# The keys' projections of a fused attention and mixture-of-experts kernel: three float32r products of split operands in place of one float32 product

## Chip, cores and metric

The kernel runs on one core of one Trainium2 chip. The metric is the device time of that core in microseconds (us), as the median of several executions. Shares of a difference are given against the 980.4 us of the kernel before.

## The reference

The reference is a chain of three parts: a linear attention with random features, a dense feed-forward layer, and a layer of eight experts with a capacity. Only the first part is touched. Cut to what matters:

```python
batch, n_heads, seq, head_dim, n_features = 4, 8, 576, 64, 128
scale = 1.0 / np.sqrt(np.sqrt(D))
def phi(x):                                       # x: q * scale or k * scale
    proj = np.einsum('bhsd,md->bhsm', x, omega)   # the projection
    sq = np.sum(x * x, axis=-1, keepdims=True) / 2.0
    h = proj - sq
    h = h - np.max(h, axis=-1, keepdims=True)
    return np.exp(h) / np.sqrt(m)
q_p, k_p = phi(q * scale), phi(k * scale)
kv = np.einsum('bhsm,bhsd->bhmd', k_p, v)
z = np.sum(k_p, axis=2)
num = np.einsum('bhsm,bhmd->bhsd', q_p, kv)
den = np.einsum('bhsm,bhm->bhs', q_p, z)[..., None] + 1e-06
attn = num / den
x = dense_layer(attn)                             # w_in, w_out: float64, 512 x 2048
return experts(x)                                 # 8 experts, 288 tokens each
```

## The kernel before

**The stages of the span.** The attention takes about the first 200 us, the dense layer runs to about 630 us, and the routing and the experts fill the rest. The work of the attention is cut into 36 units of 1024 rows (eight blocks of 128 rows of a head): 18 units of keys first, then 18 units of queries. The list `seq` (line 340) holds them in this order. So the attention has a **key stretch** and a **query stretch**.

**One unit.** `st_T` (line 208) transposes the unit's rows on TensorE (four transposes, line 212) into one bank of PSUM, the tile `tp`, and ScalarE copies it to `tH` in SBUF (line 215). GpSimd squares the rows and adds the two halves of each row's squares (lines 218 and 220). `st_TL` (line 225) has VectorE sum the squares (line 233); for a unit that is split it also forms the low part `tL` = `tp` minus `tH` on VectorE (line 230). `st_proj` (line 236) then multiplies four blocks of the transposed rows with the 128 x 256 matrix of features. If the unit has no `tL`, each block is one float32 matmul against `bdfl` (line 247). If it has one, each block is three float32r matmuls, high by high, high by low, low by high, in the helper `mm3` (lines 204 to 206) against `bdH` and `bdL`. VectorE takes the row maxima (lines 253 and 255) and forms the bias of the exponential (lines 260 and 261). ScalarE computes the exponential in eight instructions (`st_exp`, line 269). A unit of keys ends with the products of `kp` and the values into `kv` (line 279), which VectorE copies out once for every half batch (line 293). A unit of queries ends with transposes (line 301), the products with `kv` (lines 314 and 319), the division on VectorE (lines 322 to 324) and transposes back (line 333).

**What sets the order.** The loop at line 386 traces step i with the stages in the order of `ORDER` (line 30): loads, a weight conversion, the transposes of unit i + 2, the projection and the exponential of unit i, then the low part and the sum of squares of unit i + 2, then the products with the values of unit i - 1. The compiler's list scheduler turns this into one fixed order of instructions for each engine, and each engine works through its own list in order. The tile `tp` has one buffer (`PA`, line 55): the transposes of the next unit wait until every reader of the last ones is done. The transposes of the queries' results use the same bank. `tH` and `tL` have three buffers each (`TH`, line 28), the projections four banks.

**The conversions beside it.** The float64 weights of the dense layer are converted to float32 on the chip, 512 columns at a time (`conv`, line 159): one load on the queue of SP, two instructions of ScalarE (lines 172 and 173), four of VectorE (lines 174 to 177) and two of GpSimd (lines 178 and 179). Twenty-two conversions are spread over the 36 steps of the attention, about two in each three steps from step 2 on (line 363).

The lines that choose the form of the projection:

```python
tH = ap.tile([P, 512], F32 if nat else F32R, tag="tH", name="tH", bufs=TH)      # 214
if not nat:                                                                     # 228
    tL = ap.tile([P, 512], F32R, tag="tL", name="tL", bufs=TH)
    nc.vector.tensor_tensor(tL, pt, tH.bitcast(F32), ALU.subtract)
if tL is None:                                                                  # 246
    nc.tensor.matmul(o, tH[:, c], bdfl, start=True, stop=True, skip_group_check=True)
else:
    mm3(o, tH[:, c], tL[:, c], bdH, bdL)
```

Of the kernel before, what the change touches and what calls it, by code (L numbers as in the profile page):

```python
# [20 lines left out]
def fused(tc, q, k, v, omega, w_in, w_out, w_gate, w1, w2, out):  # L21
# [7 lines left out]
    L1, L2, L3, LK, TA, TB, NA = 2, 3, 4, 1, 2, 2, 4  # L29
# [20 lines left out]
    with ctx:  # L50
# [9 lines left out]
        def ps(tag):  # L60
            if tag == "big":
                turn[0] += 1
                tag = ("s8", "kv", "kv")[turn[0] % 3]
            tag = TG.get(tag, tag)
            return pp.tile([P, 512], F32, tag=tag, name=tag, bufs=PA[tag])
# [56 lines left out]
        def ensure(kind, u):  # L122
            if kind == "v":
                key = (kind, u)
                if key not in held:
                    held[key] = load_v(u)
                return held[key]
            key = (kind, u[0], u[1], u[-1])
            if key not in held:
                src = {"k": k, "q": q}[kind]  # L130
                held[key] = load_mixed(src, u[1]) if u[0] == "m" else load_full(src, u[1], u[3])
            r = held[key]
            return r if u[0] == "m" else r[:, :, 2 * u[2] * D:(2 * u[2] + 2) * D]

        def quads(u, a):

            return a.rearrange("p (a j) d -> p a j d", a=2) if u[0] == "m" else a.rearrange("p j (a d) -> p a j d", a=2)
# [43 lines left out]
        def conv_in(f, pool, pool2):  # L181
            dst = wbig[f // 8].rearrange("p (c n) -> p c n", c=4)[:, :, (f % 8) * P:(f % 8 + 1) * P]
            m = 2 if wide else 1
            conv(pool, wi_src[:, :, f * P * m:(f + 1) * P * m], dst, (4, P), pool2)

        def conv_out(f, pool, pool2=None):
            conv(pool, wo_src[:, f], wbig[2 + f // 8][:, (f % 8) * 512:(f % 8 + 1) * 512], (512,), pool2)
# [20 lines left out]
        def st_T(kind, u, nat):  # L208
            src = ensure(kind, u)
            pt = ps("T")  # L210
            for j in range(4):
                nc.tensor.transpose(pt[:, j * P:(j + 1) * P],
                                    src[:, 2 * j:2 * j + 2].rearrange("p a d -> p (a d)") if u[0] == "m" else src[:, j], ident)
            tH = ap.tile([P, 512], F32 if nat else F32R, tag="tH", name="tH", bufs=TH)
            nc.scalar.copy(tH, pt)
            sq = ap.tile([P, 2, 4, D], F32, tag="sq", name="sq", bufs=2)
            sf = quads(u, src)
            nc.gpsimd.tensor_tensor(sq, sf, sf, ALU.mult)
            s2 = ap.tile([P, 2, 4, D // 2], F32, tag="s2", name="s2", bufs=2)
            nc.gpsimd.tensor_tensor(s2, sq[:, :, :, :D // 2], sq[:, :, :, D // 2:], ALU.add)  # L220
            return pt, tH, s2, nat
# [3 lines left out]
        def st_TL(st):  # L225
            pt, tH, sq, nat = st
            tL = None
            if not nat:
                tL = ap.tile([P, 512], F32R, tag="tL", name="tL", bufs=TH)
                nc.vector.tensor_tensor(tL, pt, tH.bitcast(F32), ALU.subtract)  # L230
            ns[0] += 1
            s8 = s8s[:, ns[0] % 8 * 8:(ns[0] % 8 + 1) * 8].rearrange("p (a j) -> p a j", a=2)
            nc.vector.tensor_reduce(s8, sq, AX.X, ALU.add)
            return tH, tL, s8

        def st_proj(u, tHL):
            tH, tL, s8 = tHL
            mx = ap.tile([P, 2, 4], F32, tag="mx", name="mx", bufs=2)
            pjs = []
            for hf in range(2):  # L240
                pj = ps("proj")
                for jj in range(2):
                    j = 2 * hf + jj
                    c = slice(j * P, (j + 1) * P)
                    o = pj[:, jj * 256:(jj + 1) * 256]
                    if tL is None:
# [3 lines that stand above are left out]
                p4 = pj.rearrange("p (h m) -> p h m", h=4)  # L250
                pjs.append(p4)
                if u[0] == "m":
                    nc.vector.tensor_reduce(mx[:, hf], p4, AX.X, ALU.max)
                else:
                    nc.vector.tensor_reduce(mx[:, :, 2 * hf:2 * hf + 2].rearrange("p a j -> p j a"),
                                            p4.rearrange("p (j a) m -> p j a m", a=2), AX.X, ALU.max)
            hm = ap.tile([P, 2, 4], F32, tag="hm", name="hm", bufs=2)
            bias = ap.tile([P, 2, 4], F32, tag="bias", name="bias", bufs=2)

            nc.vector.scalar_tensor_tensor(hm, s8, -SCALE * SCALE / 2.0, mx, ALU.mult, ALU.add)  # L260
            nc.vector.scalar_tensor_tensor(bias, s8, -SCALE * SCALE / 2.0, hm, ALU.mult, ALU.subtract)  # L261
            return pjs, bias

        def st_exp(u, pb):
            pjs, bias = pb
            kp = (ap if u[0] == "f" else at_p).tile([P, 2, 4, M], F32, tag="kp" + u[0], name="kp", bufs=KP if u[0] == "f" else 2)
            for s in range(8):
                i, j = at(u, s)
                nc.scalar.activation(kp[:, i, j], pjs[s // 4][:, s % 4], AF.Exp, bias=bias[:, i, j:j + 1])  # L269
            return kp  # L270
# [13 lines left out]
        def kv_of(u):  # L284
            if u[0] == "m":
                return
            _, b, rp, hg = u
            for r in range(2):
                kv_mm(b, hg, u, r, full, rp == 0 and r == 0, False)
            if rp == 1:  # L290
                rows = slice(64 * (b % 2), 64 * (b % 2) + 64)
                kv_mm(b, hg, ("m", b // 2), hg, rows, False, True)
                nc.vector.tensor_copy(kv[b][:, 4 * hg:4 * hg + 4].rearrange("p h d -> p (h d)"), kvacc.pop((b, hg))[:, 0:260])
# [46 lines left out]
        seq = [("k", u) for u in korder] + [("q", u) for u in qorder]  # L340
        n = len(seq)
        T, pj, ex, qT, nums = {}, {}, {}, {}, {}

        def need(i):
            if 0 <= i < n:
                ensure(*seq[i])

        def need_v(i):
            if 0 <= i < n and seq[i][0] == "k":
                ensure("v", seq[i][1])  # L350
# [10 lines left out]
        def stages(i):  # L361
            yield "load", lambda: (need(i + NA), need_v(i + VF - 2))
            z = next((z for z in range(NF + CE) if C0 + int(z * CS) == i), None)
            if z is not None:
                yield "conv", lambda: conv_in(z, ar, ap) if z < NF else conv_out(z - NF, ar, ap)
            if 0 <= i + TA < n:
                yield "T", lambda: T.__setitem__(i + TA, st_T(*seq[i + TA], seq[i + TA][0] == "k"))
            if 0 <= i < n:
                yield "proj", lambda: pj.__setitem__(i, st_proj(seq[i][1], T.pop(i)))
                yield "exp", lambda: ex.__setitem__(i, st_exp(seq[i][1], pj.pop(i)))  # L370
            if 0 <= i + TB < n:
                yield "TL", lambda: T.__setitem__(i + TB, st_TL(T[i + TB]))
            if 0 <= i - LK < n and seq[i - LK][0] == "k":
                def kv_():
                    u = seq[i - LK][1]
                    kps[u], vs[u] = ex.pop(i - LK), held["v", u]
                    kv_of(u)
                yield "kv", kv_
            if 0 <= i - L1 < n and seq[i - L1][0] == "q":
                yield "qT", lambda: qT.__setitem__(i - L1, st_qT(seq[i - L1][1], ex.pop(i - L1)))  # L380
            if 0 <= i - L2 < n and seq[i - L2][0] == "q":
                yield "num", lambda: nums.__setitem__(i - L2, st_num(seq[i - L2][1], qT.pop(i - L2)))
            if 0 <= i - L3 < n and seq[i - L3][0] == "q":
                yield "xT", lambda: st_xT(seq[i - L3][1], nums.pop(i - L3))

        for i in range(-TA, n + 6):
            st = dict(stages(i))
            for name in ORDER:
                if name in st:
                    st[name]()  # L390
            if i == GI:
                gate()
# [276 lines left out]
        i = 0  # L669
# [396 lines left out]
```

## Time and profile before

| what | value |
|---|---|
| runs | 980.35, 980.4 and 984.51 us, median 980.4 us |
| the profiled execution | 981.92 us |
| its span, first to last instruction | 980.1 us |
| busy over the span | PE 92%, PEld 80%, DVE 70%, ACT 50%, POOL 50% |
| key stretch, first to last projection | 9.31 to 85.86 us |
| query stretch, first projection to the last attention unit | 85.86 to about 195 us |

PE is TensorE's matmuls, PEld its weight loads, DVE is VectorE, ACT ScalarE, POOL GpSimd and SP the engine that issues most loads. The profiled execution's time holds 1.8 us around its span. Shares over the whole span mix stages that have different limits, so the stages have to be read one by one. A matmul's duration in the profile overlaps the next one's, so the cost of a matmul in a dense row is the distance between two starts.

### The profile page before, as it was taken

The numbers are of one execution on the slowest core, as the hardware profiler recorded it, in microseconds if no ns is written. First come the engines' busy times: TensorE is split into PE (matmuls) and PEld (weight loads), VectorE is DVE, ScalarE is ACT, GpSimd is POOL, SyncE is SP. The second block draws the span as 40 slices with busy tenths as digits, with TensorE's granted clock in tenths as the row PEclk, the third lists the DMA queues.
The fourth block names the chain that finished last, engine by engine and source line by source line (L and its number), as shares of the span: only waits on it lengthen the run. The fifth ranks groups of instructions, "written<-read, shape, count | busy, mean of one in ns | idle before, by whom it ended". The sixth has DMA issues, their size and how long they took to land. (4 is left out here: it accounts for less than half of the span.)

```text
span 980.1 us, 16364 instructions
## 1 busy us (share of the span) xinstructions
PE 901.3 (92%) x5753; PEld 783.2 (80%) x5753; DVE 685.0 (70%) x1789; ACT 491.2 (50%) x1082; POOL 485.6 (50%) x447
## 2 busy tenths in 40 slices
PE   7999899999899999999999997886999899898996
PEld 6998788877678888878878886655888888787996
DVE  4779888778875662694369239967888887976442
ACT  5767788865454544534543455322344343342552
POOL 6669765346653533545444556352433533525442
PEclk9999899999999999999999999996999999998999
DMA  8855522012301000000010001014624624615500
GB/s 196 226 157 158 153 89 82 2 69 82 151 1 36 8 1 1 33 12 0 1 44 1 1 0 44 1 47 171 197 86 136 221 74 148 221 43 203 197 25 25
DMA packets 74850, 81.89 MB, mean 84 GB/s; under 512 B 27016, under 2 KB 59784, under 8 KB 74640
## 3 DMA queue, kind: packets, MB, share of 16 engines
q1 hardware_dynamic: 71696, 71.41, 22.9%
q0 software_dynamic: 3072, 9.44, 3.2%
q8 instruction: 45, 0.74, 0.3%
q14 instruction: 37, 0.30, 0.1%
HBM read 71.39 MB, written 9.45 MB: 82 GB/s over the span
## 5 line engine op out<-in xcount | busy, mean ns | idle before, releaser
L501 POOL TENSOR_TENSOR iL<-W,iH 128x512 fp32r<-128x512 f32 x80 | 114.9, 1437 | 103.7 <-ACT iH L500 88.6
L924 POOL TENSOR_TENSOR iL<-We,iH 128x512 fp32r<-128x512 f32 x63 | 84.8, 1349 | 135.2 <-ACT iH L921 127.9
L204 PE MATMUL kv<-xH,iH 128*128 128x512 f32 (+2 forms) x376 | 134.2, 357 | 5.0 <-DVE gLk L545 3.3
L206 PE MATMUL kv<-xH,iL 128*128 128x512 f32 (+2 forms) x376 | 130.0, 346 | 2.6 <-POOL iL L501 2.6
L205 PE MATMUL kv<-xL,iH 128*128 128x512 f32 (+2 forms) x376 | 130.3, 347 | 0.9 <-DVE xL L520 0.9
L509 POOL TENSOR_TENSOR oL<-W,oH 128x512 fp32r<-128x512 f32 x60 | 82.0, 1368 | 94.0 <-ACT oH L508 93.8
L578 DVE SCALAR_TENSOR_TENSOR junk<-xs,wgb 128x512 f32<-128x512 f32 x128 | 118.9, 957 | 2.3 <-PE tp L593 2.2
L204 PE MATMUL pj<-oH,gH 128*128 128x512 f32 x256 | 103.2, 403 | 3.5 <-DVE xs L569 3.5
L206 PE MATMUL pj<-oH,gL 128*128 128x512 f32 x256 | 101.8, 398 | 0.0
L205 PE MATMUL pj<-oL,gH 128*128 128x512 f32 x256 | 101.3, 396 | 0.0
L500 ACT CAST iH<-W 128x512 fp32r<-128x512 f32 x80 | 49.7, 621 | 80.4 <-PE kv L205 49.5
L269 ACT ACTIVATE kp<-pj,bias 128x128 f32<-128x128 f32 x288 | 79.1, 409 | 17.4 <-DVE bias L261 14.5
L204 PEld LDWEIGHTS kv<-xH,iH 128*128 128x128 f32 x376 | 73.0, 194 | 14.6 <-DVE gLk L545 4.2
L204 PE MATMUL pj<-hH,oH 128*128 128x288 f32 x256 | 82.7, 323 | 0.0
L206 PEld LDWEIGHTS kv<-xH,iL 128*128 128x128 f32 x376 | 73.1, 194 | 11.3 <-POOL iL L501 4.3
L921 ACT CAST iH<-We 128x512 fp32r<-128x512 f32 x64 | 39.5, 619 | 84.2 <-PE kv L205 39.3
L205 PE MATMUL pj<-hL,oH 128*128 128x288 f32 x256 | 77.0, 301 | 3.2 <-DVE hL L946 3.2
L205 PEld LDWEIGHTS kv<-xL,iH 128*128 128x128 f32 x376 | 73.3, 195 | 8.2 <-DVE xL L520 1.2
L543 DVE SCALAR_TENSOR_TENSOR kv<-r,kv 128x512 f32<-128x512 f32 (+1 forms) x54 | 34.6, 641 | 62.6 <-ACT r L542 62.3
L206 PE MATMUL pj<-hH,oL 128*128 128x288 f32 x256 | 76.8, 300 | 0.0
L178 POOL TENSOR_TENSOR stg<-cg,stg 128x512 f32<-128x512 f32 x32 | 41.7, 1303 | 70.4 <-issue 30.4
L204 PE MATMUL s<-xH,iH 128*128 128x288 f32 (+2 forms) x200 | 69.6, 348 | 2.9 <-DVE gLk L545 2.9
(418 smaller groups left out, 2374.7 us busy)
## 6 DMA issues: line engine op xcount, KB each, us to landing
We<-in_moe_w_dram SPq DMA_DIRECT2D x64, 512.0 KB, 8.8
stg<-in_moe_w_in_dram SPq DMA_DIRECT2D x16, 512.0 KB, 3.8
stg<-in_moe_w_out_dram SPq DMA_DIRECT2D x16, 512.0 KB, 3.5
ld<-in_k_dram SPq DMA_DIRECT2D x8, 512.0 KB, 5.3
vf<-in_v_dram SPq DMA_DIRECT2D x32, 128.0 KB, 3.6
ld<-in_q_dram SPq DMA_DIRECT2D x8, 512.0 KB, 5.3
xd<-xs SPq DMA_DIRECT2D x16, 256.0 KB, 2.3
wgb<-wgd SPq DMA_DIRECT2D x1, 2048.0 KB
```

What stands on the lines that cost most here:

```text
L178: nc.gpsimd.tensor_tensor(lf, g.bitcast(F32), lf, ALU.mult)
L204: nc.tensor.matmul(o, aH, bH, start=first, stop=False, skip_group_check=True)
L205: nc.tensor.matmul(o, aH, bL, start=False, stop=False, skip_group_check=True)
L206: nc.tensor.matmul(o, aL, bH, start=False, stop=last, skip_group_check=True)
L269: nc.scalar.activation(kp[:, i, j], pjs[s // 4][:, s % 4], AF.Exp, bias=bias[:, i, j:j + 1])
L500: nc.scalar.copy(iH, wi)
L501: on_pool.append(nc.gpsimd.tensor_tensor(iL, wi, iH.bitcast(F32), ALU.subtract).ins)
L509: (nc.gpsimd if (ib > 0 if ib < NB else f >= OD) else nc.vector).tensor_tensor(oL, wo, oH.bitcast(F32), ALU.subtract)
L543: nc.vector.scalar_tensor_tensor(ph[:, :n], r[:, :n], 1.0, ph[:, :n], ALU.min, ALU.mult)
L578: nc.vector.scalar_tensor_tensor(junk, x, 1.0, wgb[:, e], ALU.mult, ALU.mult, accum_out=d)
L921: nc.scalar.copy(iH, wi)
L924: (nc.vector if first and f == 0 else nc.gpsimd).tensor_tensor(iL, wi, iH.bitcast(F32), ALU.subtract)
```

## The change

The keys take the form that the queries have. `tH` of a unit of keys becomes float32r, `tL` is formed on VectorE, and each block's projection is three float32r matmuls.

```diff
@@ -364,7 +364,7 @@
             if z is not None:
                 yield "conv", lambda: conv_in(z, ar, ap) if z < NF else conv_out(z - NF, ar, ap)
             if 0 <= i + TA < n:
-                yield "T", lambda: T.__setitem__(i + TA, st_T(*seq[i + TA], seq[i + TA][0] == "k"))
+                yield "T", lambda: T.__setitem__(i + TA, st_T(*seq[i + TA], False))
             if 0 <= i < n:
                 yield "proj", lambda: pj.__setitem__(i, st_proj(seq[i][1], T.pop(i)))
                 yield "exp", lambda: ex.__setitem__(i, st_exp(seq[i][1], pj.pop(i)))
```

## Rows read from the trace of the kernel before

**Rows 1.** Busy in stretches: length, PE, PEld, DVE, ACT, POOL, granted clock, DMA, GB/s.
```profile
25.63:80.77 55.14, 54.50 (x377) 50.08 (x375) 42.81 (x99) 40.31 (x126) 38.16 (x36) 1.00 0.71 196
85.86:111.06 25.20, 20.44 (x146) 18.07 (x146) 22.80 (x51) 17.69 (x51) 20.41 (x18) 0.86 0.60 164
98.98:105.81 6.83, 4.49 (x18) 3.53 (x19) 5.69 (x12) 4.88 (x14) 4.60 (x4) 0.50 0.97 245
111.06:185.00 73.94, 68.41 (x596) 66.30 (x595) 66.71 (x200) 65.84 (x180) 40.82 (x39) 1.00 0.22 74
300.00:400.00 100.00, 100.00 (x528) 84.50 (x527) 55.11 (x115) 48.33 (x96) 40.99 (x48) 1.00 0.03 11
```

**Rows 2.** Waits from 25.63 to 80.77: waiter <- releaser, us, times, longest.
```profile
ACT kp L269 <- DVE bias L261: 10.3, 5, 3.5
...
DVE mx L255 <- PE pj L247: 6.4, 11, 1.3
DVE kv L293 <- PE kv L279: 4.9, 5, 1.3
...
PE kv L279 <- ACT kp L269: 0.5, 2, 0.3
...
DVE mx L253 <- PE pj L247: 0.3, 1, 0.3
```

**Rows 3.** TensorE in order of time, float32 projections of the keys: start, us, what.
```profile
53.06 3.19 PE L247 MATMUL pj<-bdf,tH 128*128 128x256 f32 x14
```

**Rows 4.** Line 247, all its matmuls: duration ns min/median/max, first and last start.
```profile
L247 PE MATMUL pj<-bdf,tH x144: 379/379/635, 9.3 to 85.1; 128*128 128x256 f32 x144
```

**Rows 5.** TensorE in order of time, one split projection of a unit of queries.
```profile
137.88 0.36 PE L204 MATMUL pj<-bdH,tH 128*128 128x256 f32 x1
138.09 0.28 PE L205 MATMUL pj<-bdL,tH 128*128 128x256 f32 x1
...
139.26 0.28 PE L206 MATMUL pj<-bdH,tL 128*128 128x256 f32 x1
```

**Rows 6.** The tiles tL and tp: durations ns min/median/max, first and last start.
```profile
L230 DVE TENSOR_TENSOR tL<-tp,tH x18: 671/677/692, 81.4 to 175.8; 128x512 fp32r<-128x512 f32 x18
L215 ACT COPY tH<-tp x18: 585/628/777, 7.8 to 77.7; 128x512 f32<-128x512 f32 x18
L215 ACT CAST tH<-tp x18: 585/614/698, 80.2 to 175.2; 128x512 fp32r<-128x512 f32 x18
```

**Rows 7.** Line 247 in 25.63 to 80.77: count | busy us, mean ns | idle.
```profile
L247 PE MATMUL pj<-bdf,tH 128*128 128x256 f32 x105 | 27.6, 388 | 0.0
```

**Rows 8.** All engines in order of time, the first units: start, us, what, idle before.
```profile
4.18 0.29 DVE L196 TENSOR_SCALAR bdf<-tp 64x128 f32<-64x128 f32 x1
...
5.85 0.40 ACT L200 CAST bdH<-bdf 128x256 fp32r<-128x256 f32 x1
...
7.76 0.58 ACT L215 COPY tH<-tp 128x512 f32<-128x512 f32 x1 [1.51 <-PE tp L212]
...
8.40 1.12 PE L212 MATMUL tp<-ident,ld 128*128 128x128 f32 x4 [0.68 <-ACT tH L215]
...
9.31 1.92 PE L247 MATMUL pj<-bdf,tH 128*128 128x256 f32 x4
...
10.01 0.43 DVE L233 TENSOR_REDUCE s<-s 128x8 f32<-128x256 f32 x1 [5.54 <-POOL s L220]
...
11.15 0.79 DVE L201 TENSOR_TENSOR bdL<-bdf,bdH 128x256 fp32r<-128x256 f32 x1
```

**Rows 9.** Waits of SP's queue from 25 to 111.
```profile
SPq L166 <- POOL W L179: 24.9, 8, 4.1
```

**Rows 10.** Waits from 85.86 to 111.06.
```profile
PE tp L212 <- DVE tL L230: 2.2, 1, 2.2
...
PE pj L301 <- ACT kp L269: 1.8, 1, 1.8
...
PE tp L212 <- PE pj L206: 0.6, 1, 0.6
```

**Rows 11.** Line 212 in 111.06 to 185: count | busy us, mean ns | idle.
```profile
L212 PE MATMUL tp<-ident,ld 128*128 128x128 f32 x40 | 6.0, 273 | 0.0
```

## The prediction

> **What bounds the kernel now.** I read the busy time by stretches first, because the page's shares mix three stages. The boundaries are starts of projections: 25.63 us is unit 4's, 80.77 us unit 17's (the last unit of keys) and 85.86 us the first unit of queries. In the key stretch from 25.63 to 80.77 us TensorE is busy 54.50 of 55.14 us, VectorE 42.81, ScalarE 40.31 and GpSimd 38.16 [rows 1]. So TensorE is full there, and VectorE works 78% of the time. The view of waits for the same stretch says it from the other side: VectorE stood 6.4 + 0.3 us before row maxima and 4.9 us before copies of `kv`, each time for TensorE, 11.6 of its 12.3 idle us; TensorE's own wait is 0.5 us, for the exponential [rows 1, 2]. The query stretch is different. From 111.06 to 185 us VectorE is busy 66.71 of 73.94 us (90.2%) and TensorE 68.41; from 85.86 to 111.06 us VectorE is busy 22.80 of 25.20 us (90.5%) and TensorE only 20.44 [rows 1]. There VectorE sets much of the pace. The change makes a unit of keys look like a unit of queries: it takes work from the engine that is full and gives work to the one that has 22% left.
>
> **What TensorE loses.** A row of fourteen float32 matmuls of the keys lasts 3.19 us [rows 3], and the last alone lasts 0.379 us [rows 4], so starts lie (3.19 - 0.379) / 13 = 0.216 us apart. A unit has four products, each recorded as two matmuls (144 records for 18 units [rows 4]): 8 x 0.216 = 1.73 us. In a split unit the starts from 138.09 to 139.26 us are ten steps, 0.117 us each [rows 5]; twelve matmuls are 1.40 us. The difference is 0.33 us in a unit, 5.9 us in 18 units. The first step of a split projection is longer, 138.09 - 137.88 = 0.21 us [rows 5]; if that were all extra, 18 x 0.09 = 1.7 us would go off again, which leaves 4.2 us. I take the full 0.33, since a float32 group after another kind of matmul has a long first record too (0.635 at most against 0.379 [rows 4]).
> The Trainium skill (FP8 and Floating Point Precision, TensorE Precision Notes) states that true float32 makes four passes through the array. Three products for four passes would give back a quarter of 18 x 1.73 us, 7.8 us; the rows say 19%, since a split matmul's step is a little over half a float32 record's, and the sum goes by the rows.
>
> **What VectorE gains.** Eighteen more subtractions of `tL`, 0.677 us each in the query units [rows 6], are 12.2 us. The projections in 25.63 to 80.77 us are 105 records, 13 units [rows 7]. The transposes run two steps ahead of the projections, so of the eighteen new subtractions those of units 0 to 5 come before this stretch, and twelve, 8.1 us, fall into it. VectorE then has 42.81 + 8.1 = 50.9 us to do there. TensorE has 13 x 0.33 = 4.3 us less, 50.2 us.
> How long does a stretch with two such loads take? The trace shows VectorE beside split units at 90.2% and 90.5% [rows 1]. At 90.2% the 50.9 us take 56.4 us, **1.3 us more** than the 55.14 now; TensorE would be at 89%, under the 92.5% that it reaches from 111.06 to 185 us. The bounds are TensorE's pace, -4.3 us, and all twelve subtractions on the path, +8.1 us (for all 18 units -5.9 and +12.2). I take the value by the 90%, because the longest stretch with this very mix of work shows it.
>
> **The head.** `bdL` now is needed before the first projection. `bdH` is ready at 5.85 + 0.40 us, and VectorE is idle until 10.01 us, so its 0.79 us are hidden ahead of the first `tH` at 7.76 us [rows 8]; without that cover they would cost 0.79 us. The second unit's transposes start at 8.40 us, as soon as the first `tH` is done; now they also wait for 0.68 us of `tL`, and the first projection, behind them at 9.31 us, with them: +0.7 us. Against that, the first float32 records lie (1.92 - 0.635) / 3 = 0.43 us apart [rows 4, 8], twice the later spacing, and two units at this pace save up to 1.3 us. Between -1.3 and +0.7 us I take 0.
>
> **Edits at no cost.** ScalarE writes `tH` in 0.614 us (median) as float32r and 0.628 us as float32 [rows 6]: nothing, on an engine busy 40.31 of 55.14 us. The bank `tp` is held longer, until `tL` is done; the cover is that transposes run two units ahead (the second rival is this cover gone). GpSimd and SP issue the same instructions. SP's loads of weights wait for the end of earlier conversions, eight times 24.9 us in all [rows 9], and the units' loads stand behind them; conversions that VectorE finishes later move these loads later. They are issued four steps ahead, so I count nothing; uncovered it would be one such wait, 4.1 us at most.
>
> **The sum.** 0 + 1.3 = +1.3 us at the end of the key stretch. What follows has no slack to make it up: it hangs on the last query unit, and TensorE is busy 100 of 100 us from 300 to 400 us [rows 1]. The profiled execution would go from 981.92 to 983.2 us. It stands 1.5 us above the median of its runs; the median goes from 980.4 to **981.7 us**.
>
> **Rivals.** *VectorE's gaps take the subtractions, and TensorE sets the pace.* For it: VectorE's idle time is 11.6 us of waits for TensorE [rows 2], more than the 8.1 us that come in. Then the 13 units give 4.3 us and unit 17 gives 0.3: 975.8 us. Against it: VectorE would have 50.9 us of work in 55.14 - 4.3 = 50.8 us, a full engine, and some conversions would have to slip into the query stretch, where VectorE is at 90% already. Chance 0.12.
> *The one bank of the transposes holds TensorE up.* The transposes of unit i + 1 may start only when `tL` of unit i is done, and `tL` stands in VectorE's list behind maxima, biases and conversions. TensorE works in order, so everything behind the transposes waits too. It decides from the point where VectorE comes to `tL` of one unit later than TensorE to the transposes of the next. In the five query units from 85.86 to 111.06 us TensorE waited 2.2 us for `tL` and 0.6 us in the same place for a projection [rows 10], 0.56 us per unit; for 18 units that is 10.1 us, less the 4.6 us of the first rival, +5.5 us. Then the clock: from 98.98 to 105.81 us, right after the 2.2 us of waiting, the granted clock is 0.50 of full speed, 1.2 GHz, and TensorE is busy 4.49 us of it [rows 1]; at 2.4 GHz that work is about half, so one such fall costs some 2.2 us. With one it is +7.7 us, 988.1 us; with two, 990.3 us. For it speaks that these query units have nearly the same VectorE work as the new key units; against it, that from 111.06 to 185 us the transposes never waited [rows 11], although `tL` is formed in each unit and TensorE is busy 92.5%. Chance 0.33.
> The Trainium skill (Perfetto Trace Analysis, Matmuls) asks that independent groups rotate through different PSUM banks so that the evacuation of one overlaps the next; here each evacuation gets a second reader on one bank, and the 2.2 us agree with it.
> That the change does not do what it says has no room: the form follows from one argument, and the query units run through the same lines.
>
> **How the numbers follow.** The forecast has a chance of 0.55, the faster rival 0.12, the slower one 0.33. A measurement of this kernel can tell about 0.5%, 4.9 us, from no change. The faster rival lies at the edge of that (-4.6 us), and with its head's -1.3 us beyond it: faster 0.12. The slower rival is beyond it, +5.5 to +9.9 us: slower 0.33. Same is 0.55. The forecast's own range is -4.3 us to +4.9 us, 976.1 to 985.3 us. The range over the cases reaches from the faster rival, 975.8 us, to the slower one with two falls of the clock, 990.3 us.
>
> **What would show it.** Eighteen more rows of `tL` at 0.68 us and a key projection of 1.4 us on TensorE must be there. If the step of the 90% holds, VectorE is busy about 90% between the projections of units 4 and 17, and that stretch lasts 56 to 57 us. Under 52 us the faster rival is right. If transposes wait for `tL` by more than 5 us in all, or the granted clock falls in the key stretch, it is the bank. I am wrong altogether if the time moves after 195 us, in stages that the change does not touch.

## The result, and the profile after

The changed kernel takes 992.91 us (median of 19 runs, 982.27 to 1001.71), the kernel before in the same comparison 980.35 us (19 runs, 971.65 to 988.51). The ratio is **1.0108, with a 95% interval of 1.0082 to 1.0134**: some 10.6 us slower. The ratio leaves out disturbed runs, four of them of the new kernel, so it lies below the quotient of the two medians. The forecast was 981.7 us, and the range ended at 990.3.

The profiled execution lasts 995.89 us (its span is 994.2). First, where the time arises. The exponential of unit 4 and the last copies of the attention's output mark the end of the start-up and the end of the attention.

Unit 4's exponential in ScalarE's timeline before (start, us, what, idle before):

```profile
29.31 2.17 ACT L269 ACTIVATE kp<-pj,bias 128x128 f32<-128x128 f32 x8 [0.27 <-PE kv L279]
```

and after:

```profile
34.30 2.17 ACT L269 ACTIVATE kp<-pj,bias 128x128 f32<-128x128 f32 x8 [2.76 <-DVE bias L261]
```

The last copies into the tile `xT` before (count: durations in ns min/median/max, first and last start):

```profile
L335 ACT COPY xT<-tp x2: 585/585/585, 193.7 to 195.1; 128x512 f32<-128x512 f32 x2
```

and after, with the tile `tL`, which now has 36 subtractions of 0.68 us instead of 18 [rows 6]:

```profile
L335 ACT COPY xT<-tp x2: 585/586/586, 208.5 to 209.8; 128x512 f32<-128x512 f32 x2
...
L230 DVE TENSOR_TENSOR tL<-tp,tH x36: 671/680/692, 11.4 to 190.6; 128x512 fp32r<-128x512 f32 x36
```

Unit 4's exponential is 34.30 - 29.31 = 5.0 us late, the end of the attention 209.8 - 195.1 = 14.7 us. The whole span is 994.2 - 980.1 = 14.1 us longer, so the stages after the attention added nothing. Now the stretches of the kernel before that are comparable (start-up, and unit 4's projection to the first one of a query), in the columns of [rows 1]:

```profile
0.00:10.00 10.00, 3.13 (x11) 2.41 (x12) 0.58 (x2) 2.72 (x4) 3.98 (x18) 1.00 0.71 152
10.00:20.00 10.00, 9.96 (x48) 8.18 (x48) 7.59 (x18) 5.98 (x21) 8.51 (x10) 1.00 1.07 274
...
25.63:85.86 60.23, 59.59 (x412) 54.78 (x411) 46.51 (x107) 44.96 (x138) 43.18 (x41) 1.00 0.68 188
```

And of the kernel after, with two stretches of low clock inside the last:

```profile
0.00:10.00 10.00, 2.12 (x6) 1.19 (x6) 1.00 (x3) 2.27 (x3) 4.50 (x18) 1.00 0.68 147
10.00:20.00 10.00, 8.00 (x43) 7.68 (x44) 6.50 (x13) 3.66 (x11) 6.38 (x9) 1.00 1.08 277
...
30.00:36.00 6.00, 4.81 (x39) 4.26 (x37) 6.00 (x11) 3.24 (x10) 2.70 (x2) 1.00 0.60 154
...
26.03:103.96 77.93, 71.25 (x490) 67.72 (x490) 60.32 (x131) 48.66 (x148) 50.59 (x48) 0.85 0.63 170
37.60:44.40 6.80, 6.80 (x33) 6.56 (x32) 3.00 (x9) 2.67 (x10) 4.59 (x6) 0.50 0.71 166
85.40:99.10 13.70, 13.70 (x63) 13.22 (x63) 8.16 (x22) 7.74 (x23) 9.75 (x9) 0.50 0.74 213
```

Two things changed. In the start-up TensorE does 1.0 + 2.0 us less work by 20 us than before. And in the key stretch, which goes from 60.23 to 77.93 us, the granted clock falls to 0.50, 1.2 GHz, for 6.8 us, 13.7 us and a third piece of 3.4 us (from 75.1 us): 23.9 us, where before there was none. In the pieces shown TensorE is busy all the time (6.80 of 6.80, 13.70 of 13.70): at half clock it is the pace, and by estimate about half of each such microsecond is lost. VectorE is busy 60.32 of 77.93 us, 77%, and does not bound the stretch as a whole.

What TensorE does ahead of a fall, in the timeline of the kernel after (start, us, what, idle before):

```profile
33.33 0.28 PE L206 MATMUL pj<-bdH,tL 128*128 128x256 f32 x1
34.72 0.95 PE L279 MATMUL kv<-vf,kp 128*128 128x65 f32 x4 [1.11 <-ACT kp L269]
...
36.47 0.66 PE L212 MATMUL tp<-ident,ld 128*128 128x128 f32 x4 [0.48 <-DVE tL L230]
...
58.76 0.95 PE L279 MATMUL kv<-vf,kp 128*128 128x65 f32 x4 [1.00 <-ACT kp L269]
...
83.20 0.95 PE L279 MATMUL kv<-vf,kp 128*128 128x65 f32 x4 [1.00 <-ACT kp L269]
```

The waits ahead of the falls at 37.6 and 85.4 us are 1.11 + 0.48 us and 1.00 us. Those of 1.11 and 1.00 us end with the exponential `kp`, which for unit 4 waits for VectorE's bias, that of 0.48 us with `tL`. Such a wait does not always bring a fall: after the 1.00 us before 58.76 us the clock held until 75.1 us. The view of waits from 26.03 to 103.96 us (waiter <- releaser, us, times, longest) gives the sums for the whole stretch:

```profile
ACT kp L269 <- DVE bias L261: 10.2, 4, 4.1
DVE mx L255 <- PE pj L206: 6.6, 7, 2.4
...
PE kv L279 <- ACT kp L269: 4.3, 4, 1.2
...
PE tp L212 <- issue: 1.5, 2, 0.9
...
PE tp L212 <- DVE tL L230: 0.5, 1, 0.5
```

TensorE's waits for `kp` rose from 0.5 us [rows 2] to 4.3 us; those for `tL`, the slower rival's bank, are 0.5 us here.

For one profiled pair the account closes: 5.0 us by unit 4; then 23.9 us of half clock in the key stretch and 3.4 us in the query stretch, against 6.8 us before (98.98 to 105.81 [rows 1]), 20.5 us more, half of it 10.2 us; together 15.2 of 14.7 us, with some 2 us of unexplained gains and losses inside. The experiments tell whether these two are causes.

### The profile page after: what moved, and what is told of

It reads as the page before. It is cut to its first block, busy times and chain, and to the rows that moved or that the text cites. A ratio compares the mean times of both kernels' runs of the same rounds, so it can differ in the third digit from the quotient of the medians.

```text
span 994.2 us, 16520 instructions
## 1 busy us (share of the span) xinstructions
PE 911.6 (92%) x5825; PEld 797.1 (80%) x5825; DVE 692.4 (70%) x1807; ACT 491.5 (49%) x1082; POOL 487.1 (49%) x447
```

## The experiments

Only two levels of the clock, 1.2 and 2.4 GHz, occur in these profiles, so a run's mean granted clock g gives its time at 1.2 GHz: 2 x (1 - g) x span. The table sets each variant against the runs of the kernel before on the same chip. "Clock" is half of the difference in that time, "rest" the difference of the mean times less "clock". It counts the whole kernel: in the profiles 31.5 to 58.8 us at 1.2 GHz lie behind the attention, in stages that no edit touches (44.8 us before, 52.1 after). Runs of one kernel scatter by 1 to 4 us around this split, so the standard error of a rest lies between 0.5 and 1.8 us, the more the fewer the runs. Over the changed kernel's 19 runs the time grew by 0.44 us for each microsecond at 1.2 GHz, near the half taken here. The edits below are cut to the lines that matter, and line numbers in a variant's rows can be shifted by its edit.

| variant | median us | ratio, 95% | clock | rest |
|---|---|---|---|---|
| split_no_low | 988.63 | 1.0060, 1.0023 to 1.0097 | +1.8 | +3.8 |
| low_unused | 988.45 | 1.0059, 1.0036 to 1.0083 | +0.4 | +5.7 |
| low_from_sbuf | 992.85 | 1.0110, 1.0078 to 1.0141 | +6.1 | +5.6 |
| two_banks | 1001.38 | 1.0194, 1.0160 to 1.0228 | +7.2 | +12.4 |
| bdl_on_pool | 993.02 | 1.0126, 1.0089 to 1.0163 | +7.6 | +5.3 |
| fourth_product | 984.05 | 1.0031, 1.0000 to 1.0062 | -3.0 | +7.5 |
| no_key_sums | 989.61 | 1.0117, 1.0089 to 1.0144 | +10.3 | +1.3 |
| low_first | 987.57 | 1.0092, 1.0059 to 1.0125 | +4.9 | +4.7 |
| bdl_first | 992.12 | 1.0068, 1.0035 to 1.0100 | +3.6 | +3.9 |
| four_bdl_first | 988.54 | 1.0059, 1.0036 to 1.0082 | -2.0 | +7.4 |
| one_product | 1004.04 | 1.0213, 1.0167 to 1.0260 | +34.4 | -14.3 |
| four_all | 993.18 | 1.0108, 1.0074 to 1.0142 | -2.5 | +12.5 |
| one_product_x4 | 982.43 | 0.9990, 0.9969 to 1.0010 | -1.7 | +1.1 |
| before_low_early | 982.65 | 1.0000, 0.9981 to 1.0019 | +2.7 | -2.2 |
| after_low_early | 999.58 | 1.0174, 1.0154 to 1.0195 | +10.8 | +5.7 |
| late_split | 984.56 | 1.0037, 1.0011 to 1.0063 | +4.6 | -1.3 |
| early_split | 988.32 | 1.0056, 1.0029 to 1.0083 | +1.4 | +4.7 |
| late_four | 987.07 | 1.0056, 1.0035 to 1.0077 | +3.4 | +2.5 |

### Each part alone

The form of the projection without the subtraction (split_no_low; the keys' low part is one constant tile):

```diff
+        tL0 = ap.tile([P, P], F32R, name="tL0", bufs=1)
...
-            tL = None
+            tL = tL0
```

> The keys keep the three float32r products, but their low part is a tile of zeros that is made once: the low part of the keys' transposed rows is left out, so VectorE has no new work and the bank of the transposes is held no longer than before. If the loss of the change comes from the subtraction on VectorE (its time, or the bank that it holds), this kernel is at or below the kernel before: between -6 us (TensorE sets the pace and has 0.33 us less per unit) and +2 us. If it comes from the products themselves or from a TensorE that is busy for less of the time and loses its clock, it stays at +7 to +12 us.

The subtraction without the form (low_unused, on the kernel before):

```diff
-            if not nat:
-                tL = ap.tile([P, 512], F32R, tag="tL", name="tL", bufs=TH)
-                nc.vector.tensor_tensor(tL, pt, tH.bitcast(F32), ALU.subtract)
+            tL = ap.tile([P, 512], F32R, tag="tL", name="tL", bufs=TH)
+            nc.vector.tensor_tensor(tL, pt, tH.bitcast(F32), ALU.subtract)
+            if nat:
+                tL = None
```

> The kernel before, whose units of keys keep the float32 product, with the subtraction formed for the keys too and used by nobody. VectorE has the 18 subtractions and the bank of the transposes is held for them; TensorE keeps its 1.73 us per unit. If VectorE and the bank make the loss, it is slower than the kernel before by +8 to +16 us, and the granted clock falls in the key stretch. If the split products make it, it is within 4 us of the kernel before.

Either part alone costs 0.6%, between the outcomes that its expectation allowed, and most of it is rest. Unit 4's exponential is late in both: it starts at 33.64 us in split_no_low and at 33.45 in low_unused, against 29.31 before. In low_unused this row and the first query's exponential (the last eight of thirteen, from 99.47 us) read

```profile
33.45 2.18 ACT L270 ACTIVATE kp<-pj,bias 128x128 f32<-128x128 f32 x8 [1.09 <-DVE bias L262]
...
98.22 3.49 ACT L270 ACTIVATE kp<-pj,bias 128x128 f32<-128x128 f32 x13
```

A larger part of the clock's (6.1 us in low_from_sbuf, next) came only with both together. In low_unused, from unit 4's projection to the first one of a query, the clock never fell:

```profile
28.16:93.71 65.55, 61.95 (x415) 55.38 (x415) 58.31 (x124) 47.16 (x141) 49.68 (x46) 1.00 0.69 192
```

VectorE is busy 89% there (58.31 of 65.55).

### The bank

The subtraction with its first operand from SBUF, so that the bank is free after ScalarE's copy (low_from_sbuf), and transposes that alternate between two banks (two_banks):

```diff
-                nc.vector.tensor_tensor(tL, pt, tH.bitcast(F32), ALU.subtract)
+            nc.vector.tensor_tensor(tL, tH.bitcast(F32) if nat else pt, tH.bitcast(F32), ALU.subtract)
```

```diff
-        s8s = ps("s8")
+        s8s = ap.tile([P, 64], F32, name="s8s", bufs=1)
+        tb = [0]
...
-            pt = ps("T")
+            tb[0] += 1
+            pt = ps(("T", "s8")[tb[0] % 2])
```

> The changed kernel, whose low part of the keys is formed as tH minus tH from SBUF instead of from the bank of the transposes: the keys' low part is zero, so it is left out of the result, but VectorE has an instruction of the same length and the bank is free after ScalarE's copy. If it is the bank that holds TensorE up, this is at most +3 us over the kernel before. If it is VectorE's time, it stays at +7 to +12 us.

> The changed kernel with two banks for the units' transposes in turn (the sums of squares move to SBUF, and their bank is the second one). It computes the whole result. If the one bank makes the loss, it is at most +3 us over the kernel before and the waits of the transposes for the low part are gone; if it is VectorE's time, it stays at +7 to +12 us.

The first is as slow as the change itself, the second slower. In two_banks no transpose waits for `tL` from 28 to 103 us; TensorE's waits there are

```profile
PE kv L281 <- ACT kp L271: 3.0, 4, 1.5
PE pj L205 <- ACT kp L271: 1.7, 2, 1.2
```

and the clock's part is still 7.2 us. So the bank is not what lets the clock fall in the key stretch. Two_banks lies above both expected outcomes; it also changed the order of the first instructions: TensorE did only 6.30 us of work from 10 to 20 us, and unit 0's exponential began at 20.4 instead of 17.25 us; its 12.4 us of rest hold that, but unit 4's exponential is only 5.8 us late, so not all of the rest is explained.

### The head

`bdL` on GpSimd (bdl_on_pool), and `bdL` ahead of the first two sums in VectorE's list (bdl_first):

```diff
-        nc.vector.tensor_tensor(bdL, bdfl, bdH.bitcast(F32), ALU.subtract)
+        nc.gpsimd.tensor_tensor(bdL, bdfl, bdH.bitcast(F32), ALU.subtract)
```

```diff
+        bl = nc.vector.tensor_tensor(bdL, bdfl, bdH.bitcast(F32), ALU.subtract).ins
...
+            with (tc.issue_after(bl) if ns[0] <= 2 else ExitStack()):
+                nc.vector.tensor_reduce(s8, sq, AX.X, ALU.add)
```

> The changed kernel with the one subtraction that makes bdL on GpSimd instead of VectorE; the lists of the other engines keep their order. In the changed kernel TensorE waited 2.9 us at its first low product, because on VectorE bdL stands behind two sums that wait for GpSimd. If the head's part of the loss is that wait, the first exponential starts 1 to 3 us earlier and the whole by as much, to +8 to +10 us over the kernel before; the half clock in the key stretch (23.9 us in the profile of the changed kernel) need not change. If the head is only shifted slack, nothing moves (within 1 us).

> The changed kernel with bdL made ahead of the first sum of squares in VectorE's list, so that it is ready at about 6.5 us instead of 11.4 us. In the run that moved it to GpSimd it came later still (12.9 us) and TensorE waited 4.1 us. Here the wait should be gone; the first exponential should start 1 to 4 us earlier than in the changed kernel. If the head is on the path and the clock is not disturbed, the kernel is 1 to 4 us under the changed one, at +7 to +10 us; if the half clock in the key stretch decides, it may come out anywhere from +4 to +12 us, and the time less half of its half clock is 1 to 4 us under that of the changed kernel.

They are judged by the timeline of the first microseconds after the change:

```profile
9.48 0.43 DVE L233 TENSOR_REDUCE s<-s 128x8 f32<-128x256 f32 x1 [5.19 <-POOL s L220]
10.16 0.43 DVE L233 TENSOR_REDUCE s<-s 128x8 f32<-128x256 f32 x1 [0.25 <-POOL s L220]
10.62 0.79 DVE L201 TENSOR_TENSOR bdL<-bdf,bdH 128x256 fp32r<-128x256 f32 x1
11.44 0.69 DVE L230 TENSOR_TENSOR tL<-tp,tH 128x512 fp32r<-128x512 f32 x1
11.46 0.58 PE L205 MATMUL pj<-bdL,tH 128*128 128x256 f32 x1 [2.86 <-DVE bdL L201]
...
12.27 1.05 PE L212 MATMUL tp<-ident,ld 128*128 128x128 f32 x4
```

VectorE is idle until 9.48 us as before, but in its list `bdL` and the first `tL` stand behind two sums that wait for GpSimd. TensorE waits 2.86 us for `bdL`, and the second unit's transposes begin at 12.27 instead of 8.40 us [rows 8]. On GpSimd `bdL` came later still: the wait is 4.13 us. In bdl_first that wait is gone, but the same transposes wait for the first `tL`:

```profile
10.90 1.12 PE L212 MATMUL tp<-ident,ld 128*128 128x128 f32 x4 [1.44 <-DVE tL L230]
```

Unit 0's exponential then starts at 15.9 us, unit 4's still at 32.9, and the rest is still 3.9 us. One cure out of two does not suffice. Nor is `bdL` needed for the loss: in low_unused no product of the keys reads it, and the second unit's transposes start as late, behind the first `tL`:

```profile
12.21 1.12 PE L212 MATMUL tp<-ident,ld 128*128 128x128 f32 x4 [2.40 <-DVE tL L229]
```

### VectorE's load and list

No sums of squares for the keys (no_key_sums, 0.43 us less per unit of keys), `tL` and the biases at a higher priority (low_first, which also has `bdL` on GpSimd), and the low part and sums ahead of the projection in the traced order, on both kernels (before_low_early, after_low_early):

```diff
+            if nat:
+                return tH, tL, s8z.rearrange("p (a j) -> p a j", a=2)
```

```diff
+                with tc.high_priority(offset=60):
+                    nc.vector.tensor_tensor(tL, pt, tH.bitcast(F32), ALU.subtract)
```

```diff
-ORDER = "load T proj exp TL kv qT num conv xT".split()
+ORDER = "load T TL proj exp kv qT num conv xT".split()
```

> The changed kernel without VectorE's sums of squares for the keys (18 x 0.43 us = 7.7 us of VectorE; a tile of zeros stands in for them, so the keys' half squares are left out of the result); the subtractions of tL stay. If VectorE's load is what makes TensorE wait and lose its clock, the half clock in the key stretch falls below 10 us and the kernel comes to +1 to +5 us over the kernel before. If the load is not the point, it stays at +8 to +12 us.

> The changed kernel with bdL on GpSimd, and with the low part and the bias of the exponential given a higher priority in the compiler's list scheduler, so that on VectorE they come ahead of the conversions' instructions. The work is the same. If the loss is a matter of where the new instructions stand in VectorE's list, the waits of TensorE for the exponential and the half clock shrink and it comes to +2 to +6 us over the kernel before; if it is the amount of work, it stays at +8 to +11 us.

> The kernel before with the low parts and sums traced ahead of the projections, so that the compiler's lists come out in another order with the same work. It measures what a new order alone is worth. If the 4 us of the loss that the clock does not account for are an accident of the order, this kernel may move by 2 to 6 us either way; if order matters little, it stays within 2 us of the kernel before.

> The changed kernel with the same other order: the low part of unit i + 2 is traced ahead of the projection of unit i. The work is that of the changed kernel. If the order places the subtraction badly, this is 3 us or more under the changed kernel (+7 us or less over the kernel before); if the loss does not hang on the order, it stays at +8 to +12 us, with 10 us or more of half clock in the key stretch.

With less work for VectorE the rest is 1.3 us, known to 1.7, but the clock's part grows to 10.3 us (34.1 us of half clock before the first query's exponential in the profile), and the ratio is that of the change. If VectorE's load had been the pace, this kernel would have been the faster one. The delay of the start-up did not go: TensorE's wait for `bdL` is gone and unit 0's exponential starts at 14.16 us, a microsecond earlier than before, yet unit 4's is

```profile
33.53 3.68 ACT L273 ACTIVATE kp<-pj,bias 128x128 f32<-128x128 f32 x13 [1.86 <-DVE bias L265]
```

The order is worth nothing for the kernel before and costs the changed one 0.7% more, which neither expected outcome of after_low_early allowed; low_first is not told apart from the change.

### TensorE's work

A fourth product, low by low, for the keys (fourth_product; with bdl_first's edit four_bdl_first; for the queries too four_all). Then the opposite: one float32r product per block, without a low part (one_product), and the same product issued four times, with the same result (one_product_x4):

```diff
+            if four:
+                nc.tensor.matmul(o, aL, bL, start=False, stop=False, skip_group_check=True)
```

```diff
-                        nc.tensor.matmul(o, tH[:, c], bdfl, start=True, stop=True, skip_group_check=True)
+                        for _ in range(4):
+                            nc.tensor.matmul(o, tH[:, c], bdH, start=True, stop=True, skip_group_check=True)
```

> The changed kernel with a fourth product, low by low, for the keys: 72 more float32r matmuls of 0.117 us, 8.4 us more work for TensorE and none for the others. If TensorE's time is on the path, it is 6 to 9 us slower than the changed kernel (+17 to +20 us over the kernel before). If the loss comes from TensorE standing idle in short waits and being granted half the clock after them, the extra work fills the waits, the half clock in the key stretch falls clearly below 23.9 us, and the time is within 3 us of the changed kernel or under it.

> The fourth product for the keys together with bdL first. The fourth product alone took the kernel to +0.3% over the kernel before, with a first exponential 4 us later than before. If the two add, this is at -2 to +2 us against the kernel before, with at most 7 us of half clock in the key stretch. If the head is not on the path it stays at +2 to +5 us.

> Four products for the queries too, with bdL first: 8.4 us more work for TensorE in the query stretch, where it is busy 92% and VectorE 90%. If more TensorE work there only fills waits, it equals the kernel with four products for the keys within 3 us; if TensorE's work is on the path there, it is 4 to 9 us slower than that.

> The keys' projection is one float32r product, high by high: both low parts of the keys are left out, so VectorE has the work that it has in the kernel before and TensorE has 18 x (1.73 - 0.47) = 23 us less. If TensorE's work sets the pace of the key stretch, it is faster than the kernel before by 5 to 15 us. If the granted clock decides, TensorE now waits in every unit, 20 us or more of the key stretch run at half clock, and the kernel is within 5 us of the kernel before, or slower, although nothing was added to any engine.

> The kernel with one float32r product for the keys, with that same product issued four times into the same place: the result is that of one product (both low parts of the keys are left out), VectorE has the work of the kernel before, and TensorE gets back 18 x 4 x 3 x 0.117 = 25 us of work that nobody needs. One product alone was 20 us slower than the kernel before. If the granted clock is what that lost, the repeats keep TensorE busy, the half clock in the key stretch falls from 64.9 us to under 10 us, and the kernel comes back to within 5 us of the kernel before, 15 us or more faster than with the work left out. If it is something else in the shorter products (the compiler's order, the first steps), the repeats cost time and it is at or above one product.

This is the clearest pair. One_product, windows (the first is unit 4's projection to the first of a query):

```profile
22.78:100.89 78.11, 70.31 (x374) 66.14 (x374) 49.00 (x108) 46.86 (x144) 42.14 (x41) 0.64 0.56 152
...
34.30:75.30 41.00, 36.69 (x162) 34.39 (x160) 19.92 (x49) 21.45 (x68) 20.67 (x21) 0.50 0.52 134
```

One_product_x4, nearly the same stretch (units' work alike):

```profile
26.36:86.87 60.51, 59.66 (x510) 58.67 (x509) 47.98 (x105) 43.73 (x135) 45.29 (x42) 1.00 0.68 190
```

With about 23 us less work for TensorE than before the kernel is 2.1% slower: between 34.3 and 109.4 us the clock is at 1.2 GHz for 41.0 + 23.9 us. Give TensorE the work back as useless repeats, and the clock stays at 1.00, the key stretch is that of the kernel before, and so is the time (0.9990). VectorE and ScalarE have the same work in both. Their lists come out in another order, but a new order alone moved the kernel before by 0.0% and the changed one by 0.7%, not by 2.1%. So the fall of the clock is caused by TensorE's missing work and decides the time. The extra products show it less sharply: fourth_product is the changed kernel with 8.4 us more work for TensorE, and its ratio is 1.0031 against 1.0108. The two with four products for the keys alone have a clock's part of -3.0 and -2.0 us and a rest of some 7.5 us; that the larger rest is the length of the added matmuls was not separated. The head's edit and the fourth product did not add up: four_bdl_first is at +0.6%, above what was expected. Four_all is some 5 us slower than it, so in the query stretch added work of TensorE is on the path.

### The start-up alone, and the rest alone

The last three leave the change out of the first six units of keys (late_split, and late_four with the fourth product), or keep it there alone (early_split):

```diff
-                yield "T", lambda: T.__setitem__(i + TA, st_T(*seq[i + TA], False))
+                yield "T", lambda: T.__setitem__(i + TA, st_T(*seq[i + TA], i + TA < 6))
```

```diff
+                yield "T", lambda: T.__setitem__(i + TA, st_T(*seq[i + TA], 6 <= i + TA < 18))
```

> The first six units of keys keep their one float32 product, the other twelve are split. Theory of the filling: the part of the loss that the clock does not explain, about 4 us, arises before unit 4's exponential (29.3 us before, 34.3 us after), so here that exponential starts by 30.5 us and only the clock's part is left: +5 to +8 us, a ratio of 1.005 to 1.008, with 15 us or more of half clock in the key stretch. Rival: the loss goes with the number of split units; then two thirds of the 4 us stay, and with the clock's part the ratio is about 1.010.

> The reverse: only the first six units of keys are split, the other twelve keep the float32 product. Theory of the filling: unit 4's exponential starts at 33 us or later, the key stretch from there on has no half clock and is that of the kernel before, and the ratio is 1.003 to 1.006 (+3 to +6 us). Rival: a third of the 4 us and none of the clock's part, a ratio of 1.001 to 1.002.

> The first six units float32, the other twelve split with four products (high and low by high and low), so that TensorE has more to do. If the loss is the filling and the clock and nothing else, neither is left: unit 4's exponential by 30.5 us, no half clock in the key stretch, and a ratio of 0.997 to 1.003. Rival: the subtractions of VectorE in the twelve units cost time by themselves; then it stays at 1.003 to 1.006 without any half clock in the key stretch.

Late_split, busy time from 10 to 20 us and in its stretch of low clock:

```profile
10.00:20.00 10.00, 9.96 (x54) 8.38 (x54) 8.16 (x19) 6.78 (x24) 8.92 (x12) 1.00 1.09 280
...
83.80:100.90 17.10, 17.10 (x79) 16.62 (x79) 10.64 (x26) 10.84 (x33) 10.01 (x10) 0.50 0.49 128
```

Unit 4's exponential in its timeline:

```profile
29.03 2.17 ACT L269 ACTIVATE kp<-pj,bias 128x128 f32<-128x128 f32 x8 [0.95 <-DVE bias L261]
```

Early_split, busy time from 10 to 20 us and in its first stretch of low clock:

```profile
10.00:20.00 10.00, 7.77 (x47) 7.46 (x47) 7.05 (x14) 3.83 (x11) 7.10 (x9) 1.00 1.09 279
...
90.70:100.90 10.20, 9.69 (x44) 9.54 (x45) 6.71 (x14) 3.92 (x12) 6.72 (x7) 0.50 0.42 120
```

Its unit 4 starts the exponential at 34.1 us. The two halves separate: twelve units without the first six cost 3.3 us, all of it the clock's (4.6, rest -1.3); the first six alone cost 6.1 us, and 4.7 of them are not the clock's. So the rest arises in the start-up and does not go with the number of split units. Three expectations failed in part: late_split costs less than the 5 to 8 us expected; early_split has a fall of the clock at 90.7 us all the same, within a wait of 1.17 us for the first query unit's `tL`; and late_four keeps one of 10.2 us in its profile and 2.5 us of rest. The fourth product does not keep the clock up reliably.

## Why the prediction was wrong

**The head, counted at 0.** This step failed first. It took `bdL` as hidden because VectorE is idle until 10.01 us [rows 8], and the first `tL` as 0.7 us. But an idle engine covers nothing that stands behind a waiting instruction in its list: behind two sums that wait for GpSimd, `bdL` ran at 10.62 us and `tL` at 11.44. TensorE lost 3.0 us by 20 us, then VectorE was full from 30 to 36 us (6.00 of 6.00) and unit 4's exponential waited 2.76 us for its bias. The term is +5.0 us in the profiled run and 4.7 us in early_split; the bounds were -1.3 and +0.7. Either operand alone does most of it: unit 4's exponential is 4.3 us late in split_no_low, which needs `bdL` and no `tL`, and 4.1 us in low_unused, where the bank waits for `tL` and no key product reads `bdL`. How this grows behind VectorE between units 0 and 4, most of all in no_key_sums, stays open.

**The key stretch, +1.3 us by VectorE's 90%.** At the full clock the step holds: in low_unused VectorE is busy 89%, and from unit 4's exponential to the first query's the time is 99.47 - 33.45 = 66.0 us against 94.11 - 29.31 = 64.8 before, +1.2 us. (From projection to projection it is 65.55 against 60.23 us, as the projections run ahead of their exponentials by other amounts; from unit 4's exponential to the last copy into `xT` it is +0.5 us, with 3.4 us less at 1.2 GHz.) Late_split, too, shows twelve split units that cost nothing beside the clock (rest -1.3 us). What failed is that the step had no term for TensorE's clock. The first query's exponential before, and after:

```profile
94.11 2.17 ACT L269 ACTIVATE kp<-pj,bias 128x128 f32<-128x128 f32 x8 [1.02 <-DVE bias L261]
```

```profile
112.52 2.14 ACT L269 ACTIVATE kp<-pj,bias 128x128 f32<-128x128 f32 x8
```

After the change the same stretch takes 112.52 - 34.30 = 78.2 us, 13.4 more, and half of its 23.9 us at 1.2 GHz is 12.0. In the profile of before TensorE was full, 54.50 of 55.14 us [rows 1]; the prediction read that as the limit from which work is taken. One_product_x4 shows the other side: that fullness kept the clock at 2.4 GHz. With less work in each unit and `kp` later, waits of about 1 us came in, and the clock fell; that it fell for want of work is shown by one_product and its repeats, that it fell by way of these waits is argued. The term is 10.2 us in the profiled pair. Over the runs it is about 5 us if the changed kernel's mean of 67.9 us at 1.2 GHz is set against the 57.7 us that the kernel before had in the later comparisons (51.2 to 60.8 in each, so 4 to 8 us); start-up and clock then make 10 of the measured 10.6 us.

**What TensorE loses.** The steps of 0.117 us are there, but products with the values break the projections up, and each piece starts with a longer step. By the distances of starts at 2.4 GHz in both traces a unit's projection takes 1.90 us before and 1.77 after, an estimate: some 2.4 us were saved and not 5.9, and they were worth nothing.

**The slower rival** had the right sign, and falls of the clock as its second half. Its place was wrong: the bank held TensorE up for 0.5 us in the key stretch, where the rival counted 10.1 us before the saving. Its size was wrong too: one or two falls of 2.2 us each, taken from one stretch of 6.83 us [rows 1], stood for 23.9 us at half clock, in which TensorE is full and loses some 12 us. The prediction also said that a fall of the clock in the key stretch would mean the bank. Two_banks shows that it does not.

**The faster rival** is out: nothing near 975.8 us was seen.

The Trainium skill (TensorE: Matmul & The Clock Gate, A second HAM failure mode: psum-queue depth-cycling) states that frequent short idles of TensorE between groups of matmuls make its clock swing between the two levels, with throughput lost although a single matmul at the high level lasts as long as elsewhere. The trace of the changed kernel agrees: waits of 0.5 to 1.2 us in the key stretch, and 23.9 us at the lower level. It would have been the rule against this change.

Not settled: which wait or lack of work brings a single fall, and why the clock falls in one variant and run and less in another. Both kernels scatter by about 1% from run to run with it. No variant was faster than the kernel before.

## What to carry to other kernels

Before work is taken off TensorE, ask who sets the pace once it has waits: if another engine's chain does, the clock may fall and take back more than the work saved. Judge such a change by the granted clock per stretch, and test it by adding useless matmuls. Cost a newly needed operand by its place in its engine's list, not by that engine's idle time, and read the start-up apart from the steady stretch.

## What was not expected

Useless matmuls made a kernel faster: against the kernel before, one_product has a ratio of 1.0213, the same kernel with each product issued four times 0.9990. And the clock stayed down while TensorE was busy without a gap, 13.70 of 13.70 us in the changed kernel and 17.10 of 17.10 in late_split.
